# Two chained MoE layers behind a 2-D Fourier transform: one matmul per group becomes a rank-1 term on VectorE, and half of the denominators a sum on GpSimd

## The chip, the cores and the metric

The kernel runs on one core of a Trainium2 chip. The metric is device time in microseconds (us) of one execution, from the program's start to its end. Five engines work side by side, each through its own queue in order: TensorE (PE, with its weight loads as PEld), VectorE (DVE), ScalarE (ACT), GpSimd (POOL) and SyncE (SP), which here issues the DMAs.

## The reference

```python
def _attn_ref(x):                                  # x: 2 x 3008 x 256
    X = np.fft.fft(x, axis=1)
    X = np.fft.fft(X, axis=2)
    return X.real.astype(np.float32)

def _moe_ref(x, w_in, w_out):                      # 6016 x 256, w_in 256 x 2048, w_out 2048 x 256
    h = x @ w_in
    r = np.maximum(h, 0.0)
    g = r * r
    return (g @ w_out).astype(np.float32)

def _moe2_ref(x, w_in, w_out, a, b):
    h = x @ w_in
    h2 = h * h
    h3 = h2 * h
    P = a[0] + a[1] * h + a[2] * h2 + a[3] * h3
    Q = 1.0 + np.abs(b[0]) * np.abs(h) + np.abs(b[1]) * h2
    g = P / (Q + 1e-06)
    return (g @ w_out).astype(np.float32)

# x -> _attn_ref -> _moe_ref -> _moe2_ref
```

## The kernel before

**Tiles.** The 6016 tokens are cut into 12 tiles, the first of 384 and the others of 512 tokens. All activations are held transposed (features on the partitions, tokens along the columns). A float32 product is made of three matmuls in a rounded float32 type: each operand is split into a high and a low part, and high x high, low x high and high x low are summed in PSUM. Weights of both layers are unpacked and split into such parts in the first 140 us.

**Layer 1.** Since the transform of a real input is symmetric, a tile from number 2 on needs only half of its columns: its second half of tokens is the mirror of the first. For each of the 16 chunks of 128 hidden units (a group), `h1_mm` forms two 256-column products in one PSUM bank: half `b=0` and half `b=1`, three matmuls (L743) for each. Feature 128 of x, which the mirror treats differently, enters by one more matmul (L745) with weights `w0` and the row `X0[t]`. Then `e1_b` (L778, ACT) copies the half `b=1` to SBUF, `e1_s` (L788, DVE) writes the sum and the difference of the two halves as the left and right 256 columns of `g`, `e1_relu` (L798, ACT) rectifies, `e1_gh` (L804) and `e1_g` (L808) square, `e1_lo` (L813, POOL) makes the low part, and `mm_o` (L769, PE) multiplies with the output weights into the banks o1a and o1b: 6 matmuls of 512 columns. Tiles 0 and 1 go another way (L726, L728) that has no feature-128 matmul.

**Layer 2** works on halves of a tile (256 tokens, the "subs" 1 to 22; sub 0 is the whole first tile) in groups of two chunks, so 128 x 512 again, 16 groups to a tile: 12 matmuls of h (`mm_h`, L713) into a bank, then for h in that bank

```python
u  = |b1*h|             # ACT  L831   PSUM -> SBUF
t1 = a3*h + a2          # ACT  L836   PSUM -> SBUF
w  = |(u + b0) * h|     # DVE  L842 (e2_q), ACT L846 (e2_w)
t1 = (t1*h + a1) * h    # DVE  L850 (e2_t2), L854 (e2_t3); h's bank is free after it
z  = 1/(w + q1)         # ACT  L859, L863 (reciprocal root, square)
gh = (t1 + a0) * z      # DVE  L876, rounded: the high part
m  = (w + q1) * gh      # DVE  L882, into the bank p3
e  = (t1 + a0) - m      # DVE  L889
gl = e * z              # POOL L893: the low part
```

and 12 matmuls of 256 columns (`mm_o` again, L769) into the bank o2a. The groups of the last two subs ("ALONE", "FIN") already keep q and m in h's bank.

**Banks.** PSUM has 8 banks. o1a, o1b and o2a collect outputs; p0, p1, p2 and, from tile 3 on, o2b go around for h of both layers and for the transform; p3 takes m only.

**What sets the order.** A planner in the program (`Queues.run`) gives every operation a cost, an engine, a due time (`place`) and the buffers it takes and gives back, plays the engines' queues through once and writes the instructions in the order it found. `SHIFT` is a table of numbers by tile and by kind of operation that moves due times. POOL operations, and DVE operations marked `port`, exclude one another in the plan.

## Time and profile before

| | |
|---|---|
| time, median of 3 runs | 1048.72 us (1047.89 to 1051.17) |
| time of the profiled execution | 1048.59 us |
| its span, first to last instruction | 1046.6 us |
| PE, PEld, DVE busy | 1021.6, 968.4, 998.0 us |
| ACT, POOL busy | 955.6, 495.0 us |

The profiled execution is 2.0 us longer than its span. A matmul in the trace lasts longer than the distance to the next one, since matmuls overlap in the array; the same holds, by a smaller amount, for operations of DVE and ACT. What an engine can do is therefore read from the distance between the starts of neighbouring operations, and "busy" says only that something was in flight.

### The profile page before, as it was taken

How to read it: one execution, taken by the hardware profiler on the slowest of the kernel's cores; microseconds unless marked ns; L12 is line 12 of the kernel's file. 1: busy time of each engine (PE TensorE's matmuls, PEld its weight loads, DVE VectorE, ACT ScalarE, POOL GpSimd, SP SyncE). 2: the span in 40 equal slices, each digit the busy share in tenths (PEclk: the TensorE clock that was granted, in tenths of full speed). 3: DMA queues.
4: the chain of work that ended last, by engine and by line, in shares of the span. 5: the costliest groups of instructions: out<-in, count | busy, mean ns of one | idle time of the engine just before them, and what ended most of it. 6: DMA issues, size and time to landing. Idle time of an engine off the chain costs nothing.

```text
span 1046.6 us, 20738 instructions
## 1 busy us (share of the span) xinstructions
PE 1021.6 (98%) x7538; PEld 968.4 (93%) x7538; DVE 998.0 (95%) x1789; ACT 955.6 (91%) x1921; POOL 495.0 (47%) x373
## 2 busy tenths in 40 slices
PE   9899989999999999999999999999999999999986
PEld 9889989999999999999999999999999999999985
DVE  6999999999999999999999799999999999999998
ACT  3688989999998999999999899999899989999896
POOL 0000026545555555455555645655564545555476
PEclk9999999999999999999999999999999999999999
DMA  9653500000000000000000000000000000000000
GB/s 350 215 204 111 169 1 1 9 19 12 11 12 11 12 19 3 12 11 12 11 12 11 1 11 22 1 12 16 16 11 11 2 11 12 2 11 11 1 12 21
DMA packets 26939, 36.90 MB, mean 35 GB/s; under 512 B 2349, under 2 KB 19445, under 8 KB 26837
## 3 DMA queue, kind: packets, MB, share of 16 engines
q1 hardware_dynamic: 26725, 35.19, 9.9%
q8 instruction: 59, 0.97, 0.4%
q14 instruction: 43, 0.35, 0.1%
q10 hardware_dynamic: 112, 0.39, 0.1%
HBM read 26.74 MB, written 8.80 MB: 34 GB/s over the span
## 4 chain that ended last, share of the span: by engine, by line
PE 76%; DVE 9%; ACT 9%; DMA 3%; issue 2%; POOL 1%; POOLq 0%; SPq 0%; ACTq 0%; DVEq 0%
PE o2a L769 20%; PE p L713 15%; PE o1a L769 10%; PE o1b L769 10%; PE p L743 8%; PE o2b L713 5%; PE o2b L743 2%; PE p L745 1%; DMA g<-in_dram 1%; DVE g L876 1%; DMA xt<-in_dram 1%; PE o2b L769 1%; DVE p L882 1%; ACT t L836 1%; DVE t L854 1%
## 5 line engine op out<-in xcount | busy, mean ns | idle before, releaser
L893 POOL TENSOR_TENSOR g<-t,y 128x512 fp32r<-128x512 f32 (+1 forms) x182 | 250.5, 1376 | 248.7 <-DVE t L889 182.2
L813 POOL TENSOR_TENSOR g<-g,g 128x512 fp32r<-128x512 f32 x160 | 216.3, 1353 | 285.9 <-ACT g L808 237.0
L769 PE MATMUL o2a<-g,w2hi 128*128 128x256 f32 (+1 forms) x1440 | 258.7, 280 | 6.3 <-POOL g L893 6.3
L769 PEld LDWEIGHTS o2a<-g,w2hi 128*128 128x128 f32 x1440 | 209.2, 188 | 12.6 <-POOL g L893 7.9
L769 PE MATMUL o2a<-g,w2lo 128*128 128x256 f32 (+1 forms) x720 | 143.6, 279 | 0.0
L876 DVE SCALAR_TENSOR_TENSOR g<-t,ab,y 128x512 fp32r<-128x512 f32 (+1 forms) x176 | 136.8, 780 | 4.6 <-ACT y L863 2.8
L769 PE MATMUL o1a<-g,w1hi 128*128 128x512 f32 x352 | 139.5, 396 | 0.0
L769 PE MATMUL o1b<-g,w1hi 128*128 128x512 f32 x352 | 138.3, 393 | 0.0
L882 DVE SCALAR_TENSOR_TENSOR p<-u,g 128x512 f32<-128x512 f32 (+1 forms) x176 | 132.0, 750 | 0.1
L889 DVE SCALAR_TENSOR_TENSOR t<-t,ab,p 128x512 f32<-128x512 f32 (+1 forms) x176 | 127.5, 724 | 0.3
L863 ACT ACTIVATE y<-y 128x512 f32<-128x512 f32 (+1 forms) x185 | 117.8, 637 | 1.2
L713 PE MATMUL p<-x2h,w2hi 128*128 128x256 f32 (+1 forms) x540 | 109.7, 284 | 7.3 <-DVE x1h L887 2.5
L846 ACT ACTIVATE u<-u 128x512 f32<-128x512 f32 (+1 forms) x176 | 110.3, 628 | 6.5 <-DVE u L842 6.1
L788 DVE TENSOR_TENSOR g<-p,bc 128x256 f32<-128x256 f32 x260 | 106.0, 414 | 9.7 <-POOL g L813 7.6
L804 ACT ACTIVATE g<-g 128x512 fp32r<-128x512 f32 (+1 forms) x175 | 110.1, 630 | 5.1 <-PE o1b L769 4.5
L798 ACT ACTIVATE g<-g 128x512 f32<-128x512 f32 x160 | 101.8, 637 | 13.7 <-DVE g L788 13.2
L859 ACT ACTIVATE y<-u 128x512 f32<-128x512 f32 (+1 forms) x176 | 110.9, 631 | 1.9
L808 ACT ACTIVATE g<-g 128x512 f32<-128x512 f32 (+1 forms) x175 | 110.2, 631 | 1.0
L769 PEld LDWEIGHTS o2a<-g,w2lo 128*128 128x128 f32 x720 | 109.8, 188 | 0.0
L713 PE MATMUL p<-x2h,w2lo 128*128 128x256 f32 (+1 forms) x540 | 108.3, 282 | 0.0
L713 PE MATMUL p<-x2l,w2hi 128*128 128x256 f32 (+1 forms) x540 | 108.1, 282 | 0.0
L842 DVE SCALAR_TENSOR_TENSOR u<-u,ab,p 128x512 f32<-128x512 f32 (+1 forms) x134 | 96.8, 723 | 6.1 <-ACT t L836 5.5
(265 smaller groups left out, 2768.4 us busy)
## 6 DMA issues: line engine op xcount, KB each, us to landing
g<-in_dram SPq DMA_DIRECT2D x48, 256.0 KB
xt<-in_dram SPq DMA_DIRECT2D x15, 384.0 KB
out_dram<-os SPq DMA_DIRECT2D x22, 256.0 KB
udram<-U SPq DMA_DIRECT2D x4, 640.0 KB
ut<-udram SPq DMA_DIRECT2D x10, 256.0 KB
x2h<-in_dram SPq DMA_DIRECT2D x8, 256.0 KB
x2l<-in_dram SPq DMA_DIRECT2D x8, 256.0 KB
x<-qdram SPq DMA_DIRECT2D x30, 1.0 KB
```

What stands on the lines that cost most here:

```text
L713: nc.tensor.matmul(h[:, c * n:(c + 1) * n], l[:, k, :], r[:, k], start=(q == 0), stop=(q == 5))
L769: nc.tensor.matmul(O[t][e], l[:, e * 128:(e + 1) * 128], r[:, c * n:(c + 1) * n], start=(i == 0 and q == 0 and (e == 0 or not one)), stop= ...
L804: nc.scalar.activation(out=e["gh"], in_=e["g"], func=ACTF.Square)
L808: nc.scalar.activation(out=e["g"], in_=e["g"], func=ACTF.Square)
L813: eng.tensor_tensor(out=e["gl"], in0=e["g"], in1=f32(e["gh"]), op=ALU.subtract)
L846: nc.scalar.activation(out=w, in_=w, func=ACTF.Abs)
L859: nc.scalar.activation(out=e["z"], in_=e["w"], func=ACTF.Abs_reciprocal_sqrt, bias=Q1)
L863: nc.scalar.activation(out=z, in_=z, func=ACTF.Square)
L876: nc.vector.scalar_tensor_tensor(out=e["gh"], in0=e["t1"], scalar=a0, in1=e["z"], op0=ALU.add, op1=ALU.mult)
L882: nc.vector.scalar_tensor_tensor(out=e["m"], in0=e["w"], scalar=Q1, in1=f32(e["gh"]), op0=ALU.add, op1=ALU.mult)
L889: nc.vector.scalar_tensor_tensor(out=e["t1"], in0=e["t1"], scalar=a0, in1=e["m"], op0=ALU.add, op1=ALU.subtract)
L893: (nc.vector if (t, j) in FIN else nc.gpsimd).tensor_tensor(out=e["gl"], in0=e["t1"], in1=e["z"], op=ALU.mult)
```

## The change

1. **Rank-1 term.** The matmul L745 of tiles 2 to 11 goes. The row of feature 128 is now written into row 64 of the second half's x (`q_row`, two small DMAs a tile after the transform, issued on SP), so that the six matmuls of `h1_mm` carry it, with one sign wrong in one half of the tokens. The error is a product of a vector over hidden units (`beta`, twice the difference of two weight rows) with the row over tokens (`X0[t]`, now spread over 128 partitions by one DMA a tile, `q_wide`). `e1_s` becomes three operations: DVE adds the halves (as before), DVE computes `beta * X0 + h` by a scalar_tensor_tensor of 128 x 256, and POOL subtracts the copied half from that (128 x 256, the new `s3`). The six matmuls of a group now alternate between the halves.
2. **q in the bank.** In every group of layer 2, what `e2_q` computes goes into h's bank; m replaces it there. p3 is free and joins the banks that go around (`BANKS5`), and h's bank is held until e has been computed.
3. **SUMS.** In the odd groups of subs 0 to 20 (88 groups) the denominator is a sum: ACT squares h with a scale (`e2_v`, in place of `e2_w`'s Abs) and POOL adds it to u (`e2_vw`, 128 x 512, in place of `e2_q` on DVE). There t3 is written into h's bank, and m and e into u's buffer.
4. **Buffers and order.** bc 2 to 3, u and t1 4 to 5, y 3 to 4; `SHIFT` is replaced, and a second table `ONE` moves single operations. The load of `w0` is smaller and comes after the weights of layer 1; two zero fills and three row copies of the start go.

```diff
-SLOTS = dict(xt=4, x1h=2, x1l=2, x0=2, x2h=2, x2l=2, ut=1, v=2, g=2, bc=2, g1=2, u=4, t1=4, y=3, g2=3, os=1,
+SLOTS = dict(xt=4, x1h=2, x1l=2, x0=2, x2h=2, x2l=2, ut=1, v=2, g=2, bc=3, g1=2, u=5, t1=5, y=4, g2=3, os=1,
-BANKS5 = BANKS + ("o2b",)
+BANKS5 = BANKS + ("o2b", "p3")
...
 SHIFT = {
-    ("dft", 0): 31, ("dft", 1): 195, ("dft", 2): 61, ("dft", 3): 41, ("dft", 4): 19, ("dft", 5): -7,
+    ("dft", 0): 2, ("dft", 1): 164, ("dft", 10): 23, ("dft", 11): 6, ("dft", 2): -45, ("dft", 3): -6,
...
+ONE = {
+    ("P", 21, 0): 50.0625, ("P", 21, 1): -786.5, ("P", 21, 2): 495.75, ("P", 21, 3): 479.625,
...
+    SUMS = [(t, j) for t in range(M) for j in range(len(GROUPS2[t])) if (t, j) not in ALONE + FIN and j % 2 == 1]
...
+    def q_wide(t):
+        X0[t] = x0t[t % 2]
+        nc.sync.dma_start(out=X0[t], in_=q_part(t, 2).partition_broadcast(128))
+
     def q_row(t):
-        X0[t] = x0t[t % 2]
-        k = (unit0[t] - sum(TILES[:2])) // 2
-        for row, part in ((0, 0), (32, 0), (64, 1)):
-            nc.sync.dma_start(out=f32(X0[t][row:row + 1]), in_=qdram[part:part + 1, k:k + 2].rearrange("o j n -> o (j n)"))
+        for part in range(2):
+            nc.sync.dma_start(out=f32(X1[t][part][64:65, 1, :]), in_=q_part(t, part).unsqueeze(0))
...
-            for b in range(2):
-                for q, (l, r) in enumerate(((wh, xh), (wl, xh), (wh, xl))):
-                    nc.tensor.matmul(h[:, b, c], l[:, b, :], r[:, b, :n], start=(q == 0), stop=(b == 1 and q == 2))
-                if b == 0:
-                    nc.tensor.matmul(h[:, 0, c], w0[:, i], X0[t][:, :n], start=False, stop=True)
+            for q, (l, r) in enumerate(((wh, xh), (wl, xh), (wh, xl))):
+                for b in range(2):
+                    nc.tensor.matmul(h[:, b, c], l[:, b, :], r[:, b, :n], start=(c + q + b == 0), stop=(c == gs - 1 and q == 2 and b == 1))
...
+        if part == 0:
+            nc.vector.tensor_tensor(out=g[:, 0], in0=H1[t, j][:, 0, 0], in1=b, op=ALU.add)
+        elif part == 1:
+            i = GROUPS1[t][j][0]
+            nc.vector.scalar_tensor_tensor(out=g[:, 1], in0=X0[t], scalar=beta[:, i:i + 1], in1=H1.pop((t, j))[:, 0, 0],
+                                           op0=ALU.mult, op1=ALU.add)
+        else:
+            nc.gpsimd.tensor_tensor(out=g[:, 1], in0=g[:, 1], in1=b, op=ALU.subtract)
...
+    def e2_v(t, j):
+        e = E2[t, j]
+        e["z"] = sb(tag2("y", t, j), [128, NMAX])[:, :e["n"]]
+        nc.scalar.activation(out=e["z"], in_=H2[t, j], func=ACTF.Square, scale=SCALES[3])
+
+    def e2_vw(t, j):
+        e = E2[t, j]
+        nc.gpsimd.tensor_tensor(out=e["w"], in0=e["w"], in1=e["z"], op=ALU.add)
...
-        e["w"] = H2[t, j] if (t, j) in ALONE + FIN else w
+        e["w"] = H2[t, j]
...
+        e["t3"] = H2[t, j] if (t, j) in SUMS else e["t1"]
+        nc.vector.scalar_tensor_tensor(out=e["t3"], in0=e["t1"], scalar=a1, in1=H2[t, j], op0=ALU.add, op1=ALU.mult)
```

On PE, in the middle of tile 5, before: the end of a layer-2 group (bank o2b) and the first half of a layer-1 group (bank p0) with its extra matmul; the three rows of L743 follow once more for the other half.

```order
L713 MATMUL o2b_6953<-x2h_6583,w2hi11_1106 128x256 x2
L713 MATMUL o2b_6953<-x2h_6583,w2lo11_1122 128x256 x2
L713 MATMUL o2b_6953<-x2l_6584,w2hi11_1106 128x256 x2
L743 MATMUL p0_6973<-x1h_5842,w1hi7_85 128x256
L743 MATMUL p0_6973<-x1h_5842,w1lo7_101 128x256
L743 MATMUL p0_6973<-x1l_5843,w1hi7_85 128x256
L745 MATMUL p0_6973<-x00_74,w0_73 128x256
```

In the changed kernel, the same place (x2 counts both halves):

```order
L819 MATMUL o2b_6691<-x2h_6547,w2hi3_1121 128x256 x2
L819 MATMUL o2b_6691<-x2h_6547,w2lo3_1137 128x256 x2
L819 MATMUL o2b_6691<-x2l_6548,w2hi3_1121 128x256 x2
L849 MATMUL p2_6708<-x1h_5401,w1hi6_84 128x256 x2
L849 MATMUL p2_6708<-x1h_5401,w1lo6_100 128x256 x2
L849 MATMUL p2_6708<-x1l_5402,w1hi6_84 128x256 x2
```

A layer-1 group has lost its seventh matmul and keeps the other six; over the program PE's list is 160 matmuls shorter and otherwise has the same matmuls.

On DVE, in tile 5, before (the second step of a layer-1 group and steps of four layer-2 groups):

```order
L788 TENSOR_TENSOR g_6985<-p2_6906,bc_6936 128x256
L882 SCALAR_TENSOR_TENSOR p3_7021<-u_6866,g2_6969 128x512
L876 SCALAR_TENSOR_TENSOR g2_7025<-t1_6933,ab_72,y_6971 128x512
L889 SCALAR_TENSOR_TENSOR t1_6885<-t1_6885,ab_72,p3_7021 128x512
L842 SCALAR_TENSOR_TENSOR u_7003<-u_7003,ab_72,o2b_6953 128x512
L850 TENSOR_TENSOR t1_7019<-t1_7019,o2b_6953 128x512
L842 SCALAR_TENSOR_TENSOR u_7035<-u_7035,ab_72,p1_7006 128x512
L854 SCALAR_TENSOR_TENSOR t1_7019<-t1_7019,ab_72,o2b_6953 128x512
```

In the changed kernel (the group in o2b is one of SUMS, the one in p3 is not):

```order
L997 SCALAR_TENSOR_TENSOR g2_6821<-o2b_6691,ab_72,y_6763 128x512
L891 TENSOR_TENSOR g_6827<-p0_6719,bc_6755 128x256
L894 SCALAR_TENSOR_TENSOR g_6827<-x00_74,beta_73,p0_6719 128x256
L969 TENSOR_TENSOR t1_6825<-t1_6825,p3_6780 128x512
L974 SCALAR_TENSOR_TENSOR t1_6825<-t1_6825,ab_72,p3_6780 128x512
L959 SCALAR_TENSOR_TENSOR p3_6780<-u_6807,ab_72,p3_6780 128x512
L1003 SCALAR_TENSOR_TENSOR u_6726<-u_6726,g2_6821 128x512
```

L959 (q) stands once for two groups, its result lies in the bank, and m (L1003) of the SUMS group reads and writes SBUF alone.

On ACT, in tile 5, with the semaphores that a row waits for, before (the rectifying L798 and the squares of two layer-1 groups):

```order
L798 ACTIVATE g_6632<-g_6632 128x512 [waits DVE_49]
L778 ACTIVATE bc_6654<-p2_6605 128x256 [waits PE_49]
L804 ACTIVATE g1_6656<-g_6632 128x512 [waits Activation_49]
L798 ACTIVATE g_6650<-g_6650 128x512 [waits DVE_49]
L808 ACTIVATE g_6632<-g_6632 128x512 [waits Activation_49]
```

and in the changed kernel (L980 is the reciprocal root of a SUMS group, L906 the rectifying):

```order
L980 ACTIVATE y_6538<-u_6495 128x512 [waits Pool_49]
L686 ACTIVATE x1h_6596<-p3_6582 128x2x128 [waits DMAHW3_49,PE_49]
L984 ACTIVATE y_6538<-y_6538 128x512 [waits Activation_49]
L906 ACTIVATE g_6526<-g_6526 128x512 [waits Pool_49]
L912 ACTIVATE g1_6611<-g_6526 128x512 [waits Activation_49]
L906 ACTIVATE g_6558<-g_6558 128x512 [waits Pool_49]
```

Where ACT's queue waited for DVE it now waits for POOL, 16 times a tile at L906 and 8 times at L980.

## Rows read from the trace of the kernel before

**Rows 1.** The page: busy time by engine, and the chain that ended last.
```profile
PE 1021.6 (98%) x7538; PEld 968.4 (93%) x7538; DVE 998.0 (95%) x1789; ACT 955.6 (91%) x1921; POOL 495.0 (47%) x373
...
PE 76%; DVE 9%; ACT 9%; DMA 3%; issue 2%; POOL 1%; POOLq 0%; SPq 0%; ACTq 0%; DVEq 0%
```

**Rows 2.** Stretches: from:to, length, busy us of each engine (instructions), clock, DMA.
```profile
250.00:300.00 50.00, 50.00 (x389) 48.01 (x388) 49.99 (x88) 48.44 (x97) 28.05 (x20) 1.00 0.04 12
...
950.00:1000.00 50.00, 46.39 (x358) 43.96 (x356) 49.08 (x80) 46.12 (x87) 25.95 (x21) 1.00 0.02 6
1000.00:1047.00 47.00, 36.18 (x288) 34.17 (x288) 40.97 (x69) 38.56 (x76) 32.85 (x26) 0.99 0.05 18
```

**Rows 3.** Waits of PE from 200 to 950 us, all: total, times, longest.
```profile
PE p L743 <- DVE x1l L602: 0.5, 1, 0.5
PE o2b L713 <- DVE g L788: 0.5, 1, 0.5
```

**Rows 4.** Timeline of ACT (start, duration): layer-1 outputs (L819), sub outputs (L911).
```profile
232.92 0.60 ACT L819 ACTIVATE x2h<-o1a 128x512 fp32r<-128x512 f32 x1
...
241.87 0.60 ACT L911 ACTIVATE os<-o2a 128x512 f32<-128x512 f32 x1
...
980.38 0.60 ACT L819 ACTIVATE x2h<-o1a 128x512 fp32r<-128x512 f32 x1 [0.81 <-PE o1a L769]
...
1001.28 0.67 ACT L911 ACTIVATE os<-o2a 128x512 f32<-128x512 f32 x1
```

**Rows 5.** Timeline of PE: one layer-1 group of tile 5.
```profile
399.80 0.39 PE L769 MATMUL o1b<-g,w1hi 128*128 128x512 f32 x1
400.03 0.28 PE L743 MATMUL p<-x1h,w1hi 128*128 128x256 f32 x1
...
400.37 0.28 PE L745 MATMUL p<-x,w 128*128 128x256 f32 x1
400.49 0.28 PE L743 MATMUL p<-x1h,w1hi 128*128 128x256 f32 x1
...
400.84 0.40 PE L769 MATMUL o2a<-g,w2hi 128*128 128x256 f32 x2
```

**Rows 6.** Timeline of DVE beside it.
```profile
399.38 0.74 DVE L842 SCALAR_TENSOR_TENSOR u<-u,ab,o2b 128x512 f32<-128x512 f32 x1
400.04 0.68 DVE L850 TENSOR_TENSOR t<-t,o2b 128x512 f32<-128x512 f32 x1
400.64 0.42 DVE L788 TENSOR_TENSOR g<-p,bc 128x256 f32<-128x256 f32 x1
400.97 0.74 DVE L854 SCALAR_TENSOR_TENSOR t<-t,ab,o2b 128x512 f32<-128x512 f32 x1
```

**Rows 7.** In-bank forms from 950 us on, by shape: count, busy us, mean ns, idle before.
```profile
L882 DVE SCALAR_TENSOR_TENSOR p<-p,g 128x512 f32<-128x512 f32 x9 | 6.3, 695 | 0.3
...
L846 ACT ACTIVATE p<-p 128x512 f32<-128x512 f32 x9 | 6.5, 724 | 0.0
```

**Rows 8.** Groups by shape, whole span: POOL's tensor_tensor at two widths.
```profile
L893 POOL TENSOR_TENSOR g<-t,y 128x512 fp32r<-128x512 f32 x166 | 233.1, 1404 | 228.8 <-DVE t L889 171.9 <-ACT g L798 7.5 <-ACT y L863 7.1
...
L893 POOL TENSOR_TENSOR g<-t,y 128x384 fp32r<-128x384 f32 x16 | 17.4, 1090 | 20.0 <-DVE t L889 10.2 <-ACT g L798 3.2 <-PE p L713 2.8
```

**Rows 9.** Timeline: u, t3 and e of the 62nd layer-2 group.
```profile
399.80 0.61 ACT L831 ACTIVATE u<-p 128x512 f32<-128x512 f32 x1
...
405.24 0.74 DVE L854 SCALAR_TENSOR_TENSOR t<-t,ab,p 128x512 f32<-128x512 f32 x1
...
414.83 0.73 DVE L889 SCALAR_TENSOR_TENSOR t<-t,ab,p 128x512 f32<-128x512 f32 x1
```

**Rows 10.** Waits of ACT from 200 to 950 us, the largest.
```profile
ACT g L798 <- DVE g L788: 12.7, 18, 2.5
```

**Rows 11.** Timeline: POOL and DVE at 406 us.
```profile
406.46 1.29 POOL L813 TENSOR_TENSOR g<-g,g 128x512 fp32r<-128x512 f32 x1
...
406.56 1.75 DVE L882 SCALAR_TENSOR_TENSOR p<-u,g 128x512 f32<-128x512 f32 x1
```

184 lines of the change are left out of this document (95 added, 89 removed), and 142 rows, old and new, of tables (ONE, SHIFT).

## The prediction

> **What bounds the kernel now.** I read the page's busy times and the chain first, then stretches, then who waits for whom, then single starts. PE is busy 98% of the span and holds 76% of the chain that ended last; DVE (95%) and ACT (91%) are close behind, POOL is at 47% [rows 1]. The stretches show that the span is not even: at 250 us PE has no idle time at all and DVE is at 49.99 of 50, while the last two stretches leave PE 3.6 and 10.8 us without work [rows 2]. Between 200 and 950 us all named waits of PE together are 1.0 us [rows 3]: for 750 us PE never looks up.
>
> That PE is really full, and not only marked as busy, follows from the distances between starts. A layer-1 group of seven matmuls of 256 columns takes from 400.03 to 400.84, so 0.116 us each, and one of 512 columns 0.23 us [rows 5]. A tile has 16 x 7 + 192 + 192 = 496 of the first kind and 96 of the second: 57.5 + 22.1 = 79.6 us, and about 2 us for the transform's few matmuls. What a tile takes is 83.1 us by layer 1 (nine tiles from 232.92 to 980.38) and 79.9 us by layer 2 (19 subs, two to a tile, from 241.87 to 1001.28) [rows 4], 81.5 on the mean. Count times distance gives the period with nothing left over. So in the middle of the kernel PE's list of matmuls is the time, and a matmul taken off it comes off the end, as long as the other three engines, the banks and the buffers keep up.
>
> **The matmuls that go.** 160 of them, one for each group of tiles 2 to 11. The one at 400.37 is followed at 400.49 [rows 5]: 0.12 us, against 0.116 as a seventh of the group. 160 x 0.117 = **18.7 us** (18.6 to 19.2). The other six of each group only change places among themselves: same weights, same columns, taken at nothing; were every change of half to cost PE a hundredth of a microsecond, it would be 160 x 4 x 0.01 = 6.4 us, and no row shows such a cost or such a gain.
>
> **DVE.** It loses 80 operations of 128 x 512 (and 8 of 128 x 384) like the one at 399.38, which is followed at 400.04: 0.66 us each, some 5.3 us a tile. The second half of `e1_s` becomes a scalar_tensor_tensor; at 512 columns that form takes 0.66 where a tensor_tensor takes 0.60 (400.04 to 400.64), so 0.06 more, 16 times a tile, 1.0 us; at worst it takes twice the 0.33 us of today's (400.64 to 400.97), 5.3 us a tile, and the gain would be gone [rows 6]. q, m and e in the bank: m in place took 695 ns [rows 7], no more than elsewhere, so nothing. Net -4.3 us a tile. PE's work falls by 16 x 0.117 = 1.9, to 79.6 us a tile, so DVE, at worst as full as now, gets some 2.4 us of air in each tile. None of this lies on the path while PE is full; it pays for the stalls below.
>
> **ACT.** Square takes the place of Abs in SUMS, one for one, and reads PSUM as u does. In the other half w and y read the bank: the in-bank w took 724 ns in flight [rows 7]. By starts I take no difference, since w in the tail is followed as quickly as elsewhere; if the time in flight counted it would be about 0.1 us for 16 operations a tile, 1.6 us. The work is unchanged and the period shorter: ACT's 48.4 of 50 [rows 2] have no room for more than about 3%.
>
> **POOL.** Here the work lands. A tile now has 32 operations of 1.40 us, 45 us. Added are 8 sums of 1.40 and 16 subtractions of 128 x 256. No row shows that width: proportion gives 0.70, the line through 1404 ns at 512 and 1090 at 384 gives 0.78 [rows 8]; I take 0.75 and keep both. 11.2 + 12.0 = 23.2 us, so POOL goes from 45 to 68 us of a 79.6 us tile, 86%.
>
> **What new waits cost.** Before, POOL's results went to PE alone. Now s3 and w feed ACT, and ACT's queue stands still behind a late one: behind the rectifying of one group wait the squares of another and the copies that free h's bank, and DVE and then PE wait for those. The nearest row is the same handover when DVE fed it: 18 late ones among the 144 of nine tiles, 12.7 us in all, 0.09 us a handover [rows 10]. At that price 24 handovers are 2.1 us a tile, about the room that ACT has. PE would see a part of it. For the wait that this puts on PE in the middle I have bounds, none and 1% of 750 us (7.5); nearest to DVE's row, which left PE at 1.0 us, I take 2 us. `q_row` makes h of the next tile wait for two small DMAs; the transform runs during the tile before, and SP, whose output copies queue behind them, is almost idle. Nothing for it, and up to 10 x 2 us if the transform came last.
>
> **Start and end.** The smaller w0 load takes some small work off DVE and ACT and three copies off SP, at a time when weights set the pace; a few operations on single columns come in for the root. I take zero for both ends, with 3 us each way. The end is POOL's: the order in the last stretches keeps the same operations there.
>
> **The sum**, against the profiled execution of 1048.6 us (span 1046.6 and 2.0 around it; the median of the runs is the same within 0.2): 1048.6 - 18.7 + 2 = 1031.9, so **1032 us**, within 1025 to 1038 by the bounds above.
>
> **Rival 1: the banks eat most of the gain.** Before, h's bank was free after t3; now it is held until e. In one ordinary group u began at 399.80, t3 ended at 405.98 and e at 415.56 [rows 9]: 6 us against 16. With 2 us for the matmuls ahead, 16 groups a tile hold a bank for 16 x 8 = 130 us before and 16 x 18 = 290 after at this pace; layer 1 adds about 16 x 6 = 100. That is 230 of 4 x 81.5 = 326 bank-us before, 70%, and 390 of 5 x 79.6 = 398 after, 98%. The plan must bring e closer to u to live on that, and where it does not succeed PE stands before a bank. If one of the 32 bank changes of a tile in ten comes 0.3 us late for PE, 10 x 32 x 0.1 x 0.3 = 10 us, the time is 1042. For it: the occupancy. Against it: e's delay is the plan's choice (the nine operations between u and e, at some 0.65 us each, need 6 us), and half of DVE's stalls go.
>
> **Rival 2: slower, by POOL and the port.** At 406.56 DVE's m, whose two inputs lie in SBUF, started just behind a POOL operation that ran from 406.46 to 407.75 [rows 11]. It took 1.75 us instead of some 0.70 [rows 7] and ended half a microsecond after POOL did, as if it had waited for it. The Trainium skill says the same ("SBUF — State Buffer", section "SBUF: two separate sides"): the port pair that the two share is an exclusive lock for the whole instruction. By that rule POOL and those operations of DVE share one place in time, and the event at 406 us agrees. The change halves the number of such DVE operations (8 of gh and 8 of m a tile, 16 x 0.63 = 10 us, where there were 32), but POOL's 68 us come on top: 78 us of a tile of 79.6. If one of POOL's 56 operations in five costs half of that 1.05 us, that is 56 / 5 x 0.53 = 5.9 us: the pair needs 84 us a tile, ACT waits for it in line, and ten tiles at some 2.4 us above the old period give 1048.6 + 24 = 1073. It decides at 81.5 us, so from a mean of 0.06 us lost per POOL operation. Against it: 1.40 us is a mean that already holds such stalls (the free one at 406.46 took 1.29), and by 1.30 the pair needs 40 x 1.30 + 16 x 0.70 + 10 = 73 us.
>
> **Rival 3: more than the matmuls.** DVE at 49.99 of 50 [rows 2] may also set how fast the work gets through where PE is not full, and with 40 us of work off DVE two thirds of PE's idle time in the last two stretches (14.4 us), or as much at the start, could go: 1048.6 - 18.7 - 10 = 1020.
>
> **How the numbers follow.** The forecast has 0.61, rival 1 has 0.20, rival 2 0.09, rival 3 0.10. A measurement of this kernel can tell about 0.3% (3.1 us) from no change. Faster by more: forecast, rival 3 and the better part of rival 1 (0.12), 0.83. Within 0.3%: the rest of rival 1, 0.08. Slower: 0.09. The range reaches from rival 3's time to a little past rival 1's: 1020 to 1045; left out are rival 2, the worst of rival 1 and half of rival 3.
>
> **What would show it.** Right: PE with 160 matmuls less, busy still near 98% in the middle, and its named waits there below 5 us; layer-1 outputs 81 us apart; DVE's busy time down by 45 to 60 us; POOL at 700 to 740 us; no ACT wait for POOL above 15 us in sum. Rival 1: PE waiting for e (now L1012) or for s2 at its h matmuls. Rival 2: ACT's rectifying and reciprocal root waiting for POOL, and POOL's 512-wide mean above 1.5 us. Rival 3: fewer idle us of PE before 150 and after 950. I am wrong if the middle shows PE idle by more than 2%, or if the three-input form of 256 columns takes twice 0.33.

## The result and the profile after

The changed kernel takes **1062.2 us** (median of 4, 1057.6 to 1063.6) where the kernel before takes 1049.0 beside it: a ratio of 1.011, with a 95% interval of 1.008 to 1.014. It is slower by 1.1%, and the forecast of 1032 us missed it by 30 us, outside its range. The profiled execution took 1057.6 us, with a span of 1055.8.

The page of the changed kernel, busy times and the chain, against [rows 1]:

```profile
PE 1016.3 (96%) x7378; PEld 952.9 (90%) x7378; DVE 984.8 (93%) x1710; ACT 949.5 (90%) x1922; POOL 732.3 (69%) x618
...
PE 45%; ACT 27%; DVE 19%; issue 5%; POOL 2%; DMA 2%; SPq 0%; POOLq 0%; DVEq 0%; ACTq 0%
```

The 160 matmuls are gone (7378 for 7538) and POOL stands where it was forecast (732). Two things do not fit. PE's share of the chain fell from 76% to 45%. And DVE, with 79 operations fewer (1710 for 1789), is busy only 13 us less.

Stretches of the changed kernel, from:to, length, then busy us of PE, PEld, DVE, ACT and POOL with their instructions:

```profile
0.00:150.00 150.00, 138.67 (x946) 127.90 (x947) 133.21 (x310) 110.14 (x243) 6.90 (x10) 0.99 0.54 184
150.00:200.00 50.00, 48.28 (x272) 43.38 (x271) 45.79 (x88) 45.56 (x103) 38.83 (x38) 0.99 0.02 6
200.00:950.00 750.00, 735.68 (x5428) 692.62 (x5427) 705.77 (x1150) 699.14 (x1396) 610.05 (x512) 1.00 0.04 12
```

The same long stretch of the kernel before, and in it the matmuls of x[128] alone:

```profile
200.00:950.00 750.00, 748.87 (x5639) 711.68 (x5638) 725.51 (x1236) 709.67 (x1405) 402.45 (x296) 1.00 0.03 11
...
200.00:950.00 750.00, 40.26 (x143) 26.82 (x143) 1.00 0.03 11
```

The matmuls in these 750 us are a measure of progress. Before, 5639 - 143 = 5496 of those that both kernels have; after, 5428. The changed kernel does less per microsecond although its list is shorter. PE's idle time went from 1 to 14 us. POOL is busy for 81% of the stretch instead of 54%.

All larger waits of PE from 200 to 950 us, with total, times and longest, against [rows 3]:

```profile
PE p L849 <- DVE u L1012: 4.4, 4, 2.0
PE p L819 <- DVE u L1012: 1.9, 1, 1.9
PE p L849 <- DVE g L894: 1.7, 3, 1.1
PE o2b L849 <- ACT t L953: 1.3, 1, 1.3
PE p L819 <- DVE t L1012: 1.3, 2, 1.0
PE p L849 <- DVE t L1012: 0.8, 1, 0.8
```

In all they are 13.6 us (before 1.0), and 8.4 of them end with e, the operation that gives h's bank back. That is the mark that the prediction gave for rival 1, the banks. It is the wrong name for the cause, as the next rows and the experiments show: the question is why e is late.

DVE's groups by shape, 200 to 950 us (count, busy us, mean ns): gh and m of the changed kernel with both inputs in SBUF, the same two with an input in the bank, and the new s2.

```profile
L997 DVE SCALAR_TENSOR_TENSOR g<-t,ab,y 128x512 fp32r<-128x512 f32 x74 | 78.3, 1058 | 0.9 <-PE o2a L873 0.8
L1003 DVE SCALAR_TENSOR_TENSOR u<-u,g 128x512 f32<-128x512 f32 x74 | 64.9, 876 | 0.5
L894 DVE SCALAR_TENSOR_TENSOR g<-x,beta,p 128x256 f32<-128x256 f32 x116 | 54.5, 470 | 0.0
...
L997 DVE SCALAR_TENSOR_TENSOR g<-p,ab,y 128x512 fp32r<-128x512 f32 x63 | 46.9, 744 | 5.1 <-ACT y L984 2.1 <-PE o2a L873 2.1 <-ACT u L939 0.5
...
L1003 DVE SCALAR_TENSOR_TENSOR p<-p,g 128x512 f32<-128x512 f32 x55 | 38.0, 690 | 0.7
```

One operation, two lengths: 1058 ns with two SBUF inputs and 744 with one, 876 and 690. No wait is named for the difference; it sits inside the busy time. (1.058 - 0.744) x 74 + (0.876 - 0.690) x 74 = **37 us** of DVE's time in the stretch. The two groups of the kernel before, where all of them have two SBUF inputs:

```profile
L876 DVE SCALAR_TENSOR_TENSOR g<-t,ab,y 128x512 fp32r<-128x512 f32 x152 | 120.7, 797 | 3.2 <-ACT y L863 2.4 <-DVE g L876 0.2
L882 DVE SCALAR_TENSOR_TENSOR p<-u,g 128x512 f32<-128x512 f32 x151 | 115.3, 764 | 0.0
```

By the same free lengths, (0.797 - 0.744) x 152 + (0.764 - 0.690) x 151 = 19 us. There are half as many such operations after the change, and each costs four times as much on the mean (0.25 us for 0.063). Their single durations show why. Before, 35 of the 303 took over 0.82 us, and the middle one of each group took 0.743 and 0.690, the in-bank lengths; after, 65 of 148 took over 0.82 us. One that is stalled loses about as much as before (0.54 and 0.57 us on the mean). What rose is the share that is stalled, from 12% to 44%.

What one of them looks like, and what comes of it: DVE, POOL and PE of the changed kernel at 437 us (start, duration).

```profile
437.94 1.69 DVE L997 SCALAR_TENSOR_TENSOR g<-t,ab,y 128x512 fp32r<-128x512 f32 x1
439.54 1.77 DVE L1003 SCALAR_TENSOR_TENSOR u<-u,g 128x512 f32<-128x512 f32 x1
441.24 0.41 DVE L891 TENSOR_TENSOR g<-p,bc 128x256 f32<-128x256 f32 x1
441.57 0.73 DVE L1012 SCALAR_TENSOR_TENSOR u<-p,ab,u 128x512 f32<-128x512 f32 x1
...
437.79 1.28 POOL L948 TENSOR_TENSOR u<-u,y 128x512 f32<-128x512 f32 x1
439.35 1.42 POOL L921 TENSOR_TENSOR g<-g,g 128x512 fp32r<-128x512 f32 x1 [0.27 <-POOL u L948]
...
442.36 0.51 PE L849 MATMUL p<-x1h,w1hi 128*128 128x256 f32 x2 [1.96 <-DVE u L1012]
```

Twice DVE starts an operation with two SBUF inputs just behind one of POOL (437.94 behind 437.79, 439.54 behind 439.35), and twice it is done half a microsecond after POOL is. The two microseconds lost make e end at 442.30, and PE, which needs e's bank, has waited 1.96 us. It is the event of [rows 11], two in a row, with a price on PE. The two next longest waits of PE have the same thing ahead of them: gh took 1.77 us at 247.63 before the wait of 1.92 at 250.12, and 1.80 at 573.13 before that of 1.44 at 575.65.

### The profile page after: what moved, and what is told of

Its sections match the earlier page's. It is cut to its first block, busy times and chain, and to the rows that moved or that the text cites. A ratio compares the mean times of both kernels' runs of the same rounds, so it can differ in the third digit from the quotient of the medians.

```text
span 1055.8 us, 20502 instructions
## 1 busy us (share of the span) xinstructions
PE 1016.3 (96%) x7378; PEld 952.9 (90%) x7378; DVE 984.8 (93%) x1710; ACT 949.5 (90%) x1922; POOL 732.3 (69%) x618
## 4 chain that ended last, share of the span: by engine, by line
PE 45%; ACT 27%; DVE 19%; issue 5%; POOL 2%; DMA 2%; SPq 0%; POOLq 0%; DVEq 0%; ACTq 0%
PE o2a L873 11%; PE p L819 9%; PE o1b L873 6%; PE o1a L873 6%; PE p L849 5%; ACT t L953 3%; DVE g L997 3%; PE o2b L819 3%; ACT g L912 3%; ACT u L939 3%; ACT y L984 3%; ACT y L980 3%; ACT g L906 2%; DVE t L969 2%; ACT g L916 2%
## 5 line engine op out<-in xcount | busy, mean ns | idle before, releaser
L897 POOL TENSOR_TENSOR g<-g,bc 128x256 f32<-128x256 f32 x160 | 142.5, 892 | 164.8 <-DVE g L894 156.8
L1016 POOL TENSOR_TENSOR g<-t,y 128x512 fp32r<-128x512 f32 (+1 forms) x96 | 127.3, 1326 | 24.2 <-DVE t L1012 19.5
L948 POOL TENSOR_TENSOR u<-u,y 128x512 f32<-128x512 f32 (+1 forms) x88 | 114.8, 1304 | 24.5 <-ACT y L944 23.3
L1016 POOL TENSOR_TENSOR g<-u,y 128x512 fp32r<-128x512 f32 (+1 forms) x88 | 117.4, 1334 | 18.9 <-DVE u L1012 16.7
L819 PE MATMUL p<-x2h,w2hi 128*128 128x256 f32 (+1 forms) x574 | 118.0, 287 | 8.8 <-DVE u L1012 2.8
L984 ACT ACTIVATE y<-y 128x512 f32<-128x512 f32 (+2 forms) x187 | 119.0, 645 | 0.7
L819 PE MATMUL p<-x2l,w2hi 128*128 128x256 f32 (+1 forms) x574 | 115.6, 283 | 0.2 <-DVE x2l L932 0.2
L819 PE MATMUL p<-x2h,w2lo 128*128 128x256 f32 (+1 forms) x574 | 115.5, 283 | 0.0
L969 DVE TENSOR_TENSOR t<-t,p 128x512 f32<-128x512 f32 (+1 forms) x149 | 99.0, 665 | 16.2 <-ACT t L953 9.9
L906 ACT ACTIVATE g<-g 128x512 f32<-128x512 f32 x160 | 102.6, 645 | 10.0 <-POOL g L897 9.6
L819 PEld LDWEIGHTS p<-x2h,w2hi 128*128 128x128 f32 x574 | 89.8, 189 | 16.9 <-DVE u L1012 3.3
L953 ACT ACTIVATE t<-p,ab 128x512 f32<-128x512 f32 (+1 forms) x149 | 102.9, 693 | 0.0
L939 ACT ACTIVATE u<-p 128x512 f32<-128x512 f32 (+1 forms) x148 | 87.9, 595 | 11.8 <-PE p L819 11.1
```

The source lines that it names most:

```text
L819: nc.tensor.matmul(h[:, c * n:(c + 1) * n], l[:, k, :], r[:, k], start=(q == 0), stop=(q == 5))
L897: nc.gpsimd.tensor_tensor(out=g[:, 1], in0=g[:, 1], in1=b, op=ALU.subtract)
L906: nc.scalar.activation(out=e["g"], in_=e["g"], func=ACTF.Relu)
L939: nc.scalar.activation(out=e["w"], in_=H2[t, j], func=ACTF.Abs, scale=SCALES[2 if (t, j) in SUMS else 1])
L953: nc.scalar.activation(out=e["t1"], in_=H2[t, j], func=ACTF.Identity, scale=SCALES[0], bias=a2)
L969: nc.vector.tensor_tensor(out=t1, in0=t1, in1=H2[t, j], op=ALU.mult)
```

## The experiments

Each ratio is to the kernel before, run beside it. "Stall" is the sum above: what DVE's operations with two SBUF inputs take over the length of their in-bank forms, from 200 to 950 us.

### Do the matmuls alone bring what they cost?

**e1**, the kernel before without the row's matmuls:

```diff
...
-                if b == 0:
-                    nc.tensor.matmul(h[:, 0, c], w0[:, i], X0[t][:, :n], start=False, stop=True)
...
```

> The kernel before, in its own order, without the 160 matmuls of feature 128 (tiles 2 to 11 lack that feature; nothing else differs). If PE's list sets the time, as the prediction has it: 1049 - 18.7 = 1030 us. If the other engines, at 91 to 95%, are so close behind that PE only waits for them: 1040 to 1046 us. This tells whether the first term of the sum was right by itself.

1040.8 us, ratio 0.992 (0.990 to 0.994): 9 us less, half of the 18.7. So the first term of the sum is too large even with nothing else changed.

**e6**, e1 without VectorE's q in the odd groups:

```diff
-        nc.vector.scalar_tensor_tensor(out=e["w"], in0=w, scalar=b0, in1=H2[t, j], op0=ALU.add, op1=ALU.mult)
+        if j % 2 == 0 or (t, j) in ALONE + FIN:
+            nc.vector.scalar_tensor_tensor(out=e["w"], in0=w, scalar=b0, in1=H2[t, j], op0=ALU.add, op1=ALU.mult)
```

> The kernel before, its own order, without x[128]'s 160 matmuls (as e1) and without VectorE's q in the odd groups of all tiles (some 90 operations of 0.66 us; ACT takes u in its place). The values are not the reference's. Theory (in e1 VectorE, busy 96%, kept half of the 18.7 us back): with some 59 us off VectorE the rest comes, 1029 to 1033. Rival (PE's own pace or ACT kept it): it stays at e1's 1040.8, within 1038 to 1042.

1037.6 us, ratio 0.990 (0.988 to 0.991). Near the rival: 3 us more than e1, not 10. With q's 59 us off it, DVE's stall doubled, from 20 us in e1 to 41.

**e9** and **e10**, the kernel before with lighter DVE and ACT, and the same without the row's matmuls (the edit of e1):

```diff
-        nc.scalar.activation(out=w, in_=w, func=ACTF.Abs)
+        nc.scalar.activation(out=w[:, :256], in_=w[:, :256], func=ACTF.Abs)
...
-        nc.vector.tensor_tensor(out=t1, in0=t1, in1=H2[t, j], op=ALU.mult)
+        nc.vector.tensor_tensor(out=t1[:, :256], in0=t1[:, :256], in1=H2[t, j][:, :256], op=ALU.mult)
...
```

> The kernel before, its own order, all its matmuls, but VectorE's and ScalarE's in-place steps of both layers (t2, t3, q, w, z, m, e; layer 1's rectifying and its second squaring) work on 256 of their 512 columns, so that both engines have a quarter to a third of their work less. The values are not the reference's. Theory: PE's list alone sets the time of the middle; only the ends shorten, by up to the 14 us that PE idles there: 1030 to 1045. Rival (PE's matmuls run faster once nothing else is near its limit): under 1025.

> e9 without x[128]'s 160 matmuls, as e1 is of the kernel before. The values are not the reference's. Theory (a matmul's price on PE is the 0.117 us of the prediction, and in e1 the other engines, close to their limits, kept half of it): e9 less 18.7 us, within 17 to 20. Rival (PE itself gives half back, by a slower pace of the matmuls that are left): e9 less 9 to 11 us.

1038.3 us (ratio 0.989, 0.987 to 0.992), as its theory had it, and 1023.4 us (0.975, 0.973 to 0.978): the matmuls are worth **14.9 us** once the engines beside PE have air, 80% of the 18.7, and between the two expectations. The stretch from 200 to 950 us, of e1, of e10 and of e9:

```profile
200.00:950.00 750.00, 747.78 (x5545) 705.82 (x5544) 730.85 (x1246) 713.51 (x1416) 405.78 (x298) 1.00 0.03 11
```
```profile
200.00:950.00 750.00, 748.99 (x5606) 711.63 (x5605) 580.66 (x1260) 614.72 (x1431) 405.34 (x301) 1.00 0.04 11
```
```profile
200.00:950.00 750.00, 749.60 (x5651) 713.31 (x5650) 573.04 (x1240) 605.24 (x1408) 398.41 (x296) 1.00 0.04 11
```

PE is "busy" for 748 us in e1 and 749 in e10, and yet does 5545 matmuls in one and 5606 in the other. A matmul of 256 columns is marked for 0.28 us and the next starts after 0.116 [rows 5], so a pause of up to 0.16 us between two of them never shows as idle time. That is why a PE of 98% looked like one that waits for nothing.

The 3.8 us that e10 lacks of the 18.7 lie in the pace of the matmuls that stay. From start to start in the whole run, pauses (over 0.125 and 0.245 us) and the row's own left out, 256 columns take 115.16 ns on the mean in e9 and 115.71 in e10, 512 columns 229.69 and 230.47. Over e10's 5410 and 1032 such distances that is 3.0 + 0.8 = 3.8 us, as much as is missing. So the rival of e10 was right in part: PE gives a fifth of the gain back. What sets the pace stays open (last section).

**e15**, e1 with ACT alone lightened:

```diff
-        nc.scalar.activation(out=e["g"], in_=e["g"], func=ACTF.Relu)
+        nc.scalar.activation(out=e["g"][:, :256], in_=e["g"][:, :256], func=ACTF.Relu)
...
-        nc.scalar.activation(out=z, in_=z, func=ACTF.Square)
+        nc.scalar.activation(out=z[:, :256], in_=z[:, :256], func=ACTF.Square)
```

> e1 (the kernel before without x[128]'s 160 matmuls) with only ScalarE lightened: its last square of layer 2 (z), layer 1's rectifying and second squaring work on 256 of 512 columns, some 0.21 us less in each of 48 operations a tile, 10 us a tile. The values are not the reference's. Theory (ScalarE, whose busy time and named waits fill 745 of the 750 us between 200 and 950 in e1 too, held what e6's lighter VectorE did not give): 1024 to 1031. Rival (VectorE, busy 96% in e1, or PE's slower pace holds it): 1036 to 1041.

1050.5 us (1044.1 to 1052.2), ratio 1.000 (0.999 to 1.002). The theory fell, and so did the rival: with 10 us a tile less on ACT the kernel is 10 us *slower* than e1. Also, the argument of that expectation was empty: busy time and named waits come to nearly the whole stretch also for an engine with much air (DVE in e13: 663 + 82). The trace shows one thing that grew; e15, DVE, 200 to 950 us:

```profile
L880 DVE SCALAR_TENSOR_TENSOR p<-u,g 128x512 f32<-128x512 f32 x151 | 126.8, 840 | 0.0
L874 DVE SCALAR_TENSOR_TENSOR g<-t,ab,y 128x512 fp32r<-128x512 f32 x152 | 121.2, 801 | 1.8 <-PE o2a L767 0.9 <-ACT y L861 0.4 <-ACT g L796 0.2
```

m was 767 ns in e1. The stall goes from 20 to 31 us, and DVE is busy for 735 of 750 us. So how often DVE and POOL meet is not only a matter of how much POOL has to do: POOL is as busy as in e1 (409 and 406 us), and what differs is when ACT hands over. That the 11 us more of stall are the whole of the 10 us was not tried.

### Which part of the change takes the time?

**e3**, the changed kernel in which neither gh nor m has two SBUF inputs in subs 0 to 20:

```diff
-        nc.vector.scalar_tensor_tensor(out=e["gh"], in0=e["t3"], scalar=a0, in1=e["z"], op0=ALU.add, op1=ALU.mult)
+        nc.vector.scalar_tensor_tensor(out=e["gh"], in0=H2[t, j], scalar=a0, in1=e["z"], op0=ALU.add, op1=ALU.mult)
...
-        nc.vector.scalar_tensor_tensor(out=e["m"], in0=e["w"], scalar=Q1, in1=f32(e["gh"]), op0=ALU.add, op1=ALU.mult)
+        nc.vector.scalar_tensor_tensor(out=e["m"], in0=H2[t, j] if (t, j) in SUMS else e["w"], scalar=Q1, in1=f32(e["gh"]), op0=ALU.add, op1=ALU.mult)
```

> The changed kernel in its own order; DVE's two operations with both inputs in SBUF (the high part in ordinary groups, m in SUMS groups) read h's bank in place of one of them, so none of DVE's layer-2 work in subs 0 to 20 meets POOL's port (values are wrong there, lengths and order the same). If DVE's stalls behind POOL make the change slow: 1042 to 1050 us. If only POOL's own length does, or the banks: 1055 to 1060.

**1042.6 us**, ratio 0.994 (0.992 to 0.997): some 18 us below the changed kernel, with every instruction still there and POOL's work unchanged. Groups of e3, DVE's and POOL's, 200 to 950 us:

```profile
L997 DVE SCALAR_TENSOR_TENSOR g<-p,ab,y 128x512 fp32r<-128x512 f32 x120 | 89.4, 745 | 8.0 <-ACT y L984 3.6 <-PE o2a L873 3.5 <-ACT u L939 0.5
...
L1003 DVE SCALAR_TENSOR_TENSOR u<-p,g 128x512 f32<-128x512 f32 x63 | 43.0, 682 | 0.4
```
```profile
L921 POOL TENSOR_TENSOR g<-g,g 128x512 fp32r<-128x512 f32 x145 | 187.9, 1297 | 82.7 <-issue 29.1 <-ACT g L916 22.9 <-POOL g L1016 11.5
L897 POOL TENSOR_TENSOR g<-g,bc 128x256 f32<-128x256 f32 x146 | 109.0, 747 | 20.2 <-DVE g L894 14.2 <-PE o2a L873 2.1 <-ACT g L912 1.3
```

Both sides are back at their free lengths: DVE at 745 and 682, POOL at 1297 and 747, where the changed kernel has 1356 and 886. PE's waits fall from 13.6 to 3.9 us. So the meetings cause the larger part of the miss, 18 to 20 of the 30 us, and they lengthen both engines' work.

**e4**, the changed kernel with a sixth bank for h (the two halves of layer 1's output share one bank, so the values are not the reference's; the banks are dealt out by hand after the planning):

```diff
+        six = BANKS5 + ("o1b",)
...
+                self.tag[key] = min(six, key=lambda n: until[n])
```

> The changed kernel in its own order with a sixth bank for h: from tile 2 on layer 1 sums both halves of its output into one bank (values are wrong), and the other joins the banks that go around, given out by the plan's own times. All engines have the same instructions. If the banks are short: 1035 to 1045 us, with PE's waits for e and s2 gone. If POOL and its port are the cause: 1055 to 1060, since what is late stays late.

1063.0 us, ratio 1.014 (1.011 to 1.016). PE's waits for e fall from 8.4 to 2.2 us, other waits take their place (12.2 us in all, 13.6 before), and the time stays, with the stall still at 33 us. Rival 1 is out, although PE's waits carried its name.

**e2, e11, e12**, the changed kernel with POOL's new operations cut short, both, the sums alone, the subtractions alone:

```diff
-            nc.gpsimd.tensor_tensor(out=g[:, 1], in0=g[:, 1], in1=b, op=ALU.subtract)
+            nc.gpsimd.tensor_tensor(out=g[:, 1, :32], in0=g[:, 1, :32], in1=b[:, :32], op=ALU.subtract)
...
-        nc.gpsimd.tensor_tensor(out=e["w"], in0=e["w"], in1=e["z"], op=ALU.add)
+        nc.gpsimd.tensor_tensor(out=e["w"][:, :64], in0=e["w"][:, :64], in1=e["z"][:, :64], op=ALU.add)
```

> The changed kernel in its own order, with POOL's two new operations cut to an eighth of their columns (64 of 512 in the sums, 32 of 256 in the subtractions; the rest of those columns is left unsummed). All instructions and waits stay, POOL's added work falls from about 257 us to about 60. If POOL's load and its port make the change slow: 1035 to 1042 us against 1060. If the banks are short: 1055 to 1060. If the new order as such is the poorer one: about 1060.

> The changed kernel with only GpSimd's sums cut short (64 of 512 columns), the subtractions left at 256. The values are not the reference's. With e2 (both cut, 1050.9, 11 us less than the changed kernel) it parts the two additions to GpSimd. If what counts is how long GpSimd holds the port, the sums (80 x 1.17 = 94 us less) give about as much as the subtractions (160 x 0.5 = 80 us less): 1056. If it is ScalarE's wait for a late subtraction, the sums give little: 1060 or more.

> The changed kernel with only GpSimd's subtractions cut short (32 of 256 columns), the sums left at 512. The values are not the reference's. If what counts is how long GpSimd holds the port: 1056. If it is ScalarE's wait for a late subtraction: 1051, all that e2 gave.

e2: 1050.9 us, ratio 1.002 (1.001 to 1.003), outside all three of its expectations. e11: 1049.3, 1.000 (0.999 to 1.002). e12: 1056.0, 1.006 (1.004 to 1.008). The sums are the worse of the two: cutting them gives all that cutting both gives. The subtractions give some 6 us alone and nothing on top. e12 came out at the port's price; for the sums neither price came out (1056, or 1060 and more).

**e14**, the changed kernel whose sums run in full, but are not waited for by ACT:

```diff
-        nc.gpsimd.tensor_tensor(out=e["w"], in0=e["w"], in1=e["z"], op=ALU.add)
+        nc.gpsimd.tensor_tensor(out=e["w"], in0=e["w"], in1=e["w"], op=ALU.add)
...
-        nc.scalar.activation(out=e["z"], in_=e["w"], func=ACTF.Abs_reciprocal_sqrt, bias=Q1)
+        nc.scalar.activation(out=e["z"], in_=e["z"] if (t, j) in SUMS else e["w"], func=ACTF.Abs_reciprocal_sqrt, bias=Q1)
```

> The changed kernel in which GpSimd's sums run in full (both inputs the same buffer), but ScalarE's root reads the square instead of the sum, so that ScalarE doesn't wait for GpSimd there; m still takes the sum. The values are not the reference's. Theory (the sums' harm is the port that they hold while VectorE wants it): GpSimd and the meetings are as in the changed kernel, so 1057 to 1063. Rival (their harm is that they come late to ScalarE): 1049 to 1052, as e11 with the sums cut short.

1058.8 us, ratio 1.011 (1.009 to 1.012), that of the changed kernel. So the sums do not harm by being late for ACT; with e3, what harms is that they run while DVE has an operation with two SBUF inputs.

**e5**, e2's and e3's edits together:

> The changed kernel with the edits of e2 and e3 together: the ordinary groups' gh and the SUMS groups' m take one input from h's bank (so no VectorE operation there has two SBUF inputs), and GpSimd sums 64 of 512 columns and subtracts 32 of 256. The values are not the reference's; every instruction is still there, in its place. Theory (the meetings of VectorE and GpSimd cost the time, e3 took them away): little is left for the short GpSimd to give, only ACT's waits for it (4.3 us in e3), so 1038 to 1042. Rival (GpSimd's lateness to ACT costs as much by itself): the two gains add up, 1042.6 - 11 = 1031, which is where the prediction stood.

1041.0 us, ratio 0.993 (0.991 to 0.995). The gains do not add up: without meetings, POOL's 145 us less buy under 2 us. Without meetings and with PE's shorter list the changed kernel needs 1041 us, and not 1032. e1 takes as long, in another order and with 20 us of stall.

The runs that keep the changed kernel's order and only touch POOL's or DVE's inputs, in one table (stall and POOL's busy time from 200 to 950 us):

| run | operations with two SBUF inputs | stall, us | POOL busy, us | ratio |
|---|---|---|---|---|
| the changed kernel | 148 | 37.0 | 610 | 1.011 |
| e14 | 149 | 32.3 | 590 | 1.011 |
| e12 | 149 | 29.8 | 538 | 1.006 |
| e11 | 149 | 22.4 | 537 | 1.000 |
| e2 | 150 | 20.6 | 466 | 1.002 |
| e3 | 0 | 0 | 586 | 0.994 |
| e5 | 0 | 0 | 441 | 0.993 |

In these runs the time goes with the stall and not with POOL's load: e3 has almost the load of e14. From 37 us of stall to none the time falls by 0.0168 x 1049 = 17.6 us, about half a microsecond for one of DVE's.

The stall in microseconds is not the whole account. e2 and e1 have the same matmuls and the same stall (20.6 and 20.3 us), and e2 is 10 us slower; in the stretch PE's named waits are 7.7 us in e2 and 1.8 in e1. A microsecond of stall costs the changed kernel more. It holds h's bank until e, so that a late e stops PE; that this is the reason was not tried, and no run gives the kernel before without its stalls.

**e16**, the changed kernel with ACT alone lightened (the edit of e15):

> The changed kernel with the same three ScalarE steps cut to 256 columns. The values are not the reference's; GpSimd, VectorE and PE have all their work. Theory (a meeting of GpSimd and VectorE costs because ScalarE, full, can't make up for what it then waits): more than half of the loss goes, 1035 to 1048. Rival (the meetings make VectorE itself the bound): 1055 or more.

1055.5 us, ratio 1.005 (1.004 to 1.007), the rival's number: some 6 us less, though the stall rises to 48 us. ACT's fullness is a smaller part of the loss.

### Is there a better version?

**e7** and **e8**, the changed kernel with the sums in no group, and in every fourth, planned anew (the edit of e8; e7 has `j < 0` in its place):

```diff
-    SUMS = [(t, j) for t in range(M) for j in range(len(GROUPS2[t])) if (t, j) not in ALONE + FIN and j % 2 == 1]
+    SUMS = [(t, j) for t in range(M) for j in range(len(GROUPS2[t])) if (t, j) not in ALONE + FIN and j % 4 == 1]
```

> The changed kernel with no group's denominator by GpSimd (all groups as the ordinary ones: q and m in h's bank, GpSimd has c1, c2 and the new subtraction, about 57 us a tile instead of 68); the same planner and numbers lay out the order anew. VectorE has 8 q a tile back (+5.3 us a tile), and 16 operations a tile with two SBUF inputs as before this edit, all gh. Theory (a meeting's price goes with GpSimd's share of the time, 72% instead of 86%, so some 6 us less stall, but VectorE is 5.3 us a tile fuller): 1050 to 1060. Rival (GpSimd's sum is the whole harm; layer 1's part is all gain): 1038 to 1042.

> The changed kernel with GpSimd's sum in every fourth group instead of every second (4 a tile; GpSimd about 62 us a tile, VectorE 2.6 us a tile more than after); the same planner and numbers lay out the order anew. Theory (meetings and VectorE's load trade off): between e7 and the changed kernel, 1050 to 1062. Rival (86% of GpSimd is over an edge and 78% is not): under both, 1040 to 1048.

1102.2 and 1096.7 us, ratios 1.051 (1.049 to 1.053) and 1.045 (1.043 to 1.047), with stalls of only 21 and 23 us. All four expectations missed. Other operations make another order, and the tables of numbers belong to one set of operations. Against the changed kernel e7 and e8 lose 40 and 35 us while their stall is lower; how much of that is the order, and how much the q that DVE has back, was not parted. So these two say nothing on the sums; the runs above, which keep the order, do.

**e13**, the changed kernel with neither sums nor q (the root's constants are left out here):

```diff
-        nc.scalar.activation(out=e["z"], in_=H2[t, j], func=ACTF.Square, scale=SCALES[3])
+        nc.scalar.activation(out=e["w"], in_=e["w"], func=ACTF.Square, bias=1.0)
...
-        nc.gpsimd.tensor_tensor(out=e["w"], in0=e["w"], in1=e["z"], op=ALU.add)
+        return
...
-        nc.vector.scalar_tensor_tensor(out=e["w"], in0=w, scalar=b0, in1=H2[t, j], op0=ALU.add, op1=ALU.mult)
+        return
...
-        nc.scalar.activation(out=w, in_=w, func=ACTF.Abs)
...
+        e["w"] = H2[t, j]
+        nc.scalar.activation(out=e["w"], in_=w, func=ACTF.Square, bias=1.0)
```

> The changed kernel with another form of the denominator in all groups of layer 2, computing all that the reference asks: |b1| h^2 + |b0| |h| + 1 is written as d^2 times ((r|h| + 1)^2 + k), with r, k and the numerator's coefficients worked out once from a and b (the numerator is divided by d^2 too). ScalarE takes the square of u + 1 where it had Square and Abs; VectorE's q in the ordinary groups and GpSimd's sum in the others are gone; the root's bias and m's scalar become pointers. The order of all that is left is the changed kernel's. GpSimd falls to some 57 us a tile, VectorE by 5.3 us a tile, ScalarE gains a pointer in 16 roots a tile (t1 with one takes 0.70 us where u takes 0.60, so 1.5 us a tile). Theory (the sums and their meetings with VectorE cost the time, and with them gone and VectorE lighter PE's shorter list shows): 1036 to 1044. Rival (ScalarE, now some 965 us, is the next bound, or the meetings of the subtraction are enough): 1046 to 1056.

1054.1 us, ratio 1.005 (1.004 to 1.007): the rival. It beats the changed kernel by some 6 us and not the kernel before. Its stretch, and two of ACT's groups:

```profile
200.00:950.00 750.00, 742.70 (x5482) 699.98 (x5481) 662.70 (x1085) 717.89 (x1409) 512.07 (x442) 1.00 0.04 12
```
```profile
L986 ACT ACTIVATE y<-u,ab 128x512 f32<-128x512 f32 x75 | 56.1, 748 | 0.0
...
L986 ACT ACTIVATE y<-p,ab 128x512 f32<-128x512 f32 x56 | 39.6, 708 | 0.3
```

DVE now has air (663 of 750 us, and it waits 58 us for ACT), while ACT, at 718, is fuller than in any other run: the root takes 748 and 708 ns with a pointer for its bias where it took 648 and 615. The Trainium skill gives about 93 ns for such an operand ("ScalarE: Activation LUTs", section "What ACT_TABLE_LOAD costs"); these rows agree, with 100 and 93. The meetings are still there too (149 operations, 25 us). Which of the two holds e13 was not told apart.

**e17** and **e18**, with t2 gone, ACT's Abs gone, and the denominator as (u + c) u by VectorE in the ordinary groups, or in all. In e18 the values are not the reference's: nothing makes the root of a SUMS group wait for the product, and one of the 88 starts ahead of it.

```diff
-        nc.scalar.activation(out=e["t1"], in_=H2[t, j], func=ACTF.Identity, scale=SCALES[0], bias=a2)
+        nc.scalar.activation(out=e["t1"], in_=H2[t, j], func=ACTF.Square, bias=a2)
...
-        nc.vector.scalar_tensor_tensor(out=e["w"], in0=w, scalar=b0, in1=H2[t, j], op0=ALU.add, op1=ALU.mult)
+        nc.vector.scalar_tensor_tensor(out=e["w"], in0=u, scalar=ab[:, 7:8], in1=u, op0=ALU.add, op1=ALU.mult)
...
-        nc.vector.tensor_tensor(out=t1, in0=t1, in1=H2[t, j], op=ALU.mult)
+        return
...
```

> The changed kernel's order with fewer operations in layer 2, computing all that the reference asks: numerator and denominator are divided by a3 (its sign goes into the output copy's scale), ScalarE's t1 becomes the square of h + a2/2 and VectorE's t2 is gone; the ordinary groups' denominator is VectorE's (u + c) u where q was, and ScalarE's Abs there is gone; in the SUMS groups it is ScalarE's closed square as in e13, without GpSimd's sum. Against the changed kernel, a tile: VectorE 16 operations less (some 10 us), ScalarE 8 less but 24 pointers more (some 3 us less), GpSimd 11 us less, 8 more VectorE operations with two SBUF inputs. Theory (ScalarE and the meetings held the change back): 1028 to 1040. Rival (the 24 meetings a tile cost as the 16 did, or ScalarE is still full): 1045 to 1055.

> e17 with the SUMS groups' denominator also by VectorE ((u + c) u in t2's place), so that ScalarE has four operations a group and not five in all 16 groups: some 9 us a tile less than the changed kernel; VectorE has 80 operations a tile instead of 88, of which 32 have two SBUF inputs. It computes all that the reference asks. Theory (ScalarE is what PE's shorter list runs into): as e17 or below, 1025 to 1035. Rival (meetings with GpSimd are the bound): above e17, 1042 to 1055.

1090.4 us (ratio 1.039, 1.037 to 1.041) and 1118.5 us (1.065, 1.063 to 1.067): with the least work on the engines two of the four slowest kernels, beyond even the rivals. DVE's three largest groups with two SBUF inputs in e17, 200 to 950 us:

```profile
L1019 DVE SCALAR_TENSOR_TENSOR g<-t,ab,y 128x512 fp32r<-128x512 f32 x73 | 68.8, 942 | 9.6 <-ACT y L1006 9.5
L980 DVE SCALAR_TENSOR_TENSOR p<-u,ab 128x512 f32<-128x512 f32 x63 | 68.5, 1088 | 1.5
L1025 DVE SCALAR_TENSOR_TENSOR u<-u,ab,g 128x512 f32<-128x512 f32 x72 | 67.9, 943 | 0.3
```

The new one takes 1088 ns, and the stall is 56 us in e17 and 88 in e18. Both go the way of the meetings. That the rest of their loss has the same cause was not tried; an order that does not fit, as may be in e7, is as possible. No version was found that computes the reference and beats the kernel before.

## Why the prediction was wrong, point by point

The 30 us between 1032 and 1062 have two parts. Without the meetings the time is 18 to 20 us lower (e3), and the 10 that are left are as many as e1 lacks of the 18.7.

**What bounds the kernel.** Half right. PE is the bound of the kernel before: e9, with much lighter DVE and ACT, does 5651 matmuls in the 750 us where the kernel before does 5639. But "PE never looks up" was read as "the others have room", and that does not follow. DVE and ACT had none to speak of.

**The matmuls that go: the first failed step.** The term of 18.7 us "comes off the end, as long as the other three engines keep up". The row's own distance was sized rightly, 0.118 us on the mean of all 160. With the others as they are the term measured 9 us (e1), with both relieved 14.9 (e10 against e9). Relieving one at a time gave 3 us (e6) or lost 10 (e15). The condition stood in the text, but no number of the sum was put on it. The 3.8 us that e10 still lacks are the slower pace of the other matmuls, which the prediction took at nothing.

**DVE: the second failed step, and the larger one.** s2 was sized rightly: the next instruction starts 0.39 us behind it, as estimated. The 80 q went. But the sum "net -4.3 us a tile" left out the operations that stay: their stall in the stretch rose from 19 to 37 us, some 2 us a tile, and DVE's busy time fell by 13 us instead of 45 to 60. The air that was to pay for all stalls was half spent before it was there.

**ACT.** Right in its size (949.5 us for 955.6). In-bank w and y take 608 and 615 ns, less than the 637 and 641 from SBUF in the kernel before.

**POOL.** Right in its size: 732 us of 700 to 740. A free subtraction takes 747 ns (e3) where 0.75 was estimated; with the meetings it takes 886.

**New waits.** The 2 us, with bounds of 0 and 7.5, were sized by the handover to ACT. ACT's waits for POOL are indeed small in the stretch, 13.0 us of which the rectifying has most:

```profile
ACT g L906 <- POOL g L897: 8.9, 14, 1.5
...
ACT y L980 <- POOL u L948: 3.6, 4, 1.3
```

and e14 shows that those of y cost nothing. The wait that counts has no name in the trace and lies in DVE's operations. PE's 13.6 us are beyond the bound of 7.5, and without the meetings 3.9 are left (e3). Neither of the prediction's last two signs of being wrong appeared: PE's idle time in the middle is 14 of 750 us, 1.9% where it named 2%, and s2 does not take twice 0.33.

**Start and end.** The start is about within the 3 us: 946 matmuls in the first 150 us, where the kernel before has 967 of the same; the 21 are some 2.4 us at 0.116. e5, without meetings, has 953.

**Rival 1, the banks.** Its mark appeared (8.4 us of PE's waits end with e) and its cause did not (e4). A wait names the last link of a chain.

**Rival 2, POOL and the port.** Its meetings happened, at a chance of 0.09, but not its path, ACT waiting in line for POOL, nor its 1073 us. Both marks that it was given failed: no ACT wait for POOL above 15 us, and POOL's 512-wide mean at 1.36 and not above 1.5. The price was looked for on POOL, which has room, and DVE, which has little, paid as much. Its point of decision, 0.06 us lost per POOL operation, was passed. Measured against e3's lengths, a tile's 56 POOL operations lose 16 x 0.06 + 16 x 0.14 + 16 x 0.04 + 8 x 0.03 = 4.1 us, 0.07 each, and DVE's 16 lose 16 x 0.25 = 4 us besides. The argument against it, that the mean of 1.40 already held such stalls, was the error: it held those of an order in which they were rare, 35 of 303 of DVE's operations. Halving their number said nothing on how many of the rest would meet POOL. The rule that the prediction cited, of an exclusive lock on the port pair ("SBUF — State Buffer", section "SBUF: two separate sides", in the Trainium skill), agrees with e3: with no DVE operation of that kind, both engines run at their free lengths.

**Rival 3.** Nothing of it; at 950 us the changed kernel is already behind.

## What to carry to other kernels

Where GpSimd runs beside VectorE operations with two SBUF inputs, compare one line's mean with that of its form with an input in PSUM: the difference times the count is a stall that no list of waits shows. It can grow when GpSimd is given more, even though fewer VectorE operations are left to meet it: here from 19 to 37 us with half as many. Work taken off a full engine is worth its time only as far as the next engines are shown to have room; here that was half. And a kernel whose order was fitted to one set of operations is to be tried with that order kept: the two that were planned anew came out 35 and 40 us slower, and could not be read.
